# Splitting float64 weights: the sign carried by a parametric ReLU and a bound on GpSimd, instead of a pass on VectorE

## Chip, core and metric

The kernel runs on one core of a Trainium2 chip. The metric is the device time of one execution in microseconds (us); smaller is better.

## What is computed

A scan over chunks of 32 steps (4 batches, 8 heads, 768 steps, head dimension 32, state 16), and behind it two feed-forward layers on 3072 tokens, 256 to 2048 to 256:

```python
y   = scan(x, a, B, C)                      # per head: CB * decay on the chunk, state between chunks
x   = y.transpose(0, 2, 1, 3).reshape(3072, 256)
h   = x @ w_in;  g = np.maximum(0.01 * h, h);  x = g @ w_out
h   = np.maximum(x @ w2_in, 0.0);              out = h * h @ w2_out
```

The four weight matrices arrive as float64, 512 Ki numbers each. The kernel reads them as 64-bit words and makes two float32 parts of each number itself, a high part that TensorE takes as it is and a low part that is the rest.

## The kernel before

**Scan.** The work is cut into 12 pieces of 256 steps. `scan_piece` computes one: scaled fp16 parts of its inputs on ScalarE and VectorE, block-diagonal copies (`diag`), products on TensorE (lines 340, 341, 365 to 367, 385, 386), running products on VectorE (lines 188, 194, 212). Its last two steps give the tokens of the feed-forward layers: `yh` on ScalarE (line 389) and then `yl` on VectorE (line 390), the instruction that the first matmuls of a block wait for.

**Feed-forward.** The tokens stand in 8 blocks of one or two pieces, and `ORDER` lists the 16 phases (layer and block: first layer of block 0, of 1, of 2, second layer of block 0, and so on). In each phase `Phase.hmm` multiplies with two or one 128-column parts of the first matrix (lines 417 to 419), `act` applies the nonlinearity on ScalarE (lines 427, 428 or 430, 432) and VectorE (line 431, and `gl` in line 433), and `omm` multiplies with the second matrix, one to three rounds later (lines 445, 446, 450).

**Weights.** The four matrices are split into 8 chunks each, 32 in all; a chunk is 128 partitions x 512 numbers. `w_step` moves four chunks on by one stage each:

- `load_w` (line 120): a DMA from SP's queue into a buffer `wst` of 64-bit words.
- `split_w`: two ScalarE instructions in place. Line 129 multiplies the upper word, read as float32, by 2 to the -112, which rebases the exponent; line 132 turns the lower word into the last bits of the fraction.
- `split_w1`: two VectorE instructions in place. Line 140 shifts the scaled upper word left by 3 and puts it over the lower word; line 141 puts the sign bit of the upper word over that, since the shift has pushed it out.
- `split_w2`: the high part on ScalarE (line 152), the low part on VectorE (line 153).

```python
nc.scalar.activation(w1.bitcast(F32), w1.bitcast(F32), AF.Copy, scale=2.0**-112)                       # 129
nc.vector.scalar_tensor_tensor(w0, w1, 3, w0, ALU.logical_shift_left, ALU.bitwise_or)                  # 140
nc.vector.scalar_tensor_tensor(w0, w1, -(1 << 31), w0, ALU.bitwise_and, ALU.bitwise_or)                # 141
```

Eight `w_step`s are written ahead of the first block; the rest is spread over the phases. In which order the instructions stand on each engine is decided at build time by a scheduler with a cost table of its own; each engine then runs its list in order, and waits by semaphores. GpSimd only sets up constants at the start (lines 68 to 88).

Of the kernel before, what the change touches and what calls it, by code (L numbers as in the profile page):

```python
# [8 lines left out]
F32 = mybir.dt.float32  # L9
F32R = mybir.dt.float32r  # L10
F16 = mybir.dt.float16
I32 = mybir.dt.int32
I64 = mybir.dt.int64
U32 = mybir.dt.uint32
AF = mybir.ActivationFunctionType
ALU = mybir.AluOpType
# [28 lines left out]
def ssd_moe_kernel(ctx: ExitStack, tc: tile.TileContext, in1, in2, w1i, w1o, w2i, w2o, out):  # L45
# [6 lines left out]
    nc = tc.nc  # L52
# [18 lines left out]
    nc.scalar.activation(lr, ones, AF.Lrelu)  # L71
    delta = cp.tile([P, U, T], F16, name="delta")


    xbh = cp.tile([P, U, 4, T], F16, name="xbh")
    xbl = cp.tile([P, U, 4, T], F16, name="xbl")
    kbd = cp.tile([P, U, 4, T], F16, name="kbd")
    sbd = cp.tile([P, U, 4, T], F16, name="sbd")
    d1e = cp.tile([P, U, T], F32, name="d1e")
# [30 lines left out]
    def load_w():  # L110
        nm, c = wq.pop(0)
        if nm == "2o" and c >= 5:
            st = yp.tile([P, 2, 256], I64, tag="y2", name="wst")
        else:
            st = wp.tile([P, 2, 256], I64, tag="w", name="wst")
        if nm[1] == "i":
            sl = (slice(None), slice(None), slice(c * 256, c * 256 + 256))
        else:
            sl = (slice(None), slice(2 * c, 2 * c + 2), slice(None))
        nc.sync.dma_start(st, w_dram[nm][sl])  # L120
        w_loaded.append((nm, c, sl, st))

    def split_w():
        nm, c, sl, st = w_loaded.pop(0)
        v = st.bitcast(I32).rearrange("p k (f two) -> p k f two", two=2)
        w0, w1 = v[:, :, :, 0], v[:, :, :, 1]


        nc.scalar.activation(w1.bitcast(F32), w1.bitcast(F32), AF.Copy, scale=2.0**-112)


        nc.scalar.activation(
            w0, w0.bitcast(U32), AF.Copy, scale=2.0**-29 * (1 - 2.0**-14), bias=7.5 * 2.0**-14 - 0.5
        )
        w_half.append((nm, c, sl, w0, w1))

    def split_w1():

        nm, c, sl, w0, w1 = w_half.pop(0)
        nc.vector.scalar_tensor_tensor(w0, w1, 3, w0, ALU.logical_shift_left, ALU.bitwise_or)  # L140
        nc.vector.scalar_tensor_tensor(w0, w1, -(1 << 31), w0, ALU.bitwise_and, ALU.bitwise_or)  # L141
        w_full.append((nm, c, sl, w0.bitcast(F32)))

    def split_w2():
# [10 lines left out]
    def w_step():  # L155
        if w_full:
            split_w2()
        if w_half:
            split_w1()
        if w_loaded:  # L160
            split_w()
        if wq:
            load_w()
# [61 lines left out]
    def piece_scales(p, tiles):  # L225
# [16 lines left out]
        iss = sm.tile([P, 1], F32, tag="iss", name="iss", bufs=3)  # L242
        nc.vector.tensor_single_scalar(er.bitcast(I32), rb.bitcast(I32), MASK, ALU.bitwise_and)
        nc.vector.tensor_scalar(ss.bitcast(I32), er.bitcast(I32), -1.0, 268.0 * E23, ALU.mult, ALU.add)
        nc.vector.tensor_scalar(iss.bitcast(I32), er.bitcast(I32), -14.0 * E23, None, ALU.add)
        kk = sm.tile([P, 1], F32, tag="kk", name="kk")
# [30 lines left out]
    def powers(mx):  # L277
# [14 lines left out]
        nc.vector.tensor_scalar(eb, Sf[:, P : P + 3], 2.0**-50, None, ALU.max)  # L292
        nc.vector.tensor_single_scalar(eb.bitcast(I32), eb.bitcast(I32), MASK, ALU.bitwise_and)
        nc.vector.tensor_scalar(sc.bitcast(I32), eb.bitcast(I32), -1.0, 267.0 * E23, ALU.mult, ALU.add)
        nc.vector.tensor_scalar(isc.bitcast(I32), eb.bitcast(I32), -13.0 * E23, None, ALU.add)
# [4 lines left out]
    def scan_piece(p, tiles, get_y):  # L300
# [12 lines left out]

        him = sp.tile([P, U, T], F16, tag="f0", name="him")
        ch = sp.tile([P, U, T], F16, tag="f2", name="ch")
# [174 lines left out]
    for _ in range(W_AHEAD):  # L490
        load_w()
# [120 lines left out]
```

## Time and profile before

| what | value |
|---|---|
| median of 3 runs | 652.51 us (652.01 to 653.04) |
| profiled execution, first to last instruction (span) | 647.8 us |
| median less that span | 4.7 us |
| busy in the span: TensorE (PE), VectorE (DVE) | 592.5 us, 420.4 us |
| busy in the span: ScalarE (ACT), GpSimd (POOL) | 356.9 us, 5.1 us |
| mean granted clock of TensorE | 0.989 |

The profile gives one execution, and of its time the span alone. Times in it count from the span's start. SP only issues DMAs. A busy TensorE is one with a matmul in flight; the start-to-start distance of its matmuls says at which of its two clock levels it works.

### The profile page before, as it was taken

What the parts mean: (1) busy time and instruction counts of PE and PEld (TensorE: products, weight loads), DVE (VectorE), ACT (ScalarE), POOL (GpSimd) and SP (SyncE); (2) the same over time, 40 slices, a digit from 0 to 9 for tenths busy, and PEclk for the clock granted to TensorE, in tenths of its full rate; (3) what the DMA queues carried; (4) which work ended last, traced back from release to release, by engine and by line L of the source; (5) the groups of instructions that cost most, each with busy time, mean ns of one, the idle gap of its engine ahead of it and who ended that gap; (6) DMA issues with size and microseconds to landing.
All of it is one profiled execution on the core that took longest, in us unless ns stands there. A gap on an engine that the chain in (4) does not pass through costs nothing.

```text
span 647.8 us, 11305 instructions
## 1 busy us (share of the span) xinstructions
PE 592.5 (91%) x4440; PEld 514.8 (79%) x4440; DVE 420.4 (65%) x726; ACT 356.9 (55%) x630; POOL 5.1 (1%) x14
## 2 busy tenths in 40 slices
PE   0278695999999999999999999999999999999997
PEld 0177595999999988899987888888888888788885
DVE  7989999898768854576554586563565322554553
ACT  5999776665555545545535555455544433544442
POOL 3000000000000000000000000000000000000000
PEclk9999898899999999999999999999999999999999
DMA  9775765423635422202212212212000000000000
GB/s 323 240 242 136 238 138 150 127 61 65 172 33 149 76 73 24 50 34 42 50 50 25 50 33 25 50 66 25 8 1 10 33 0 1 0 1 2 32 2 32
DMA packets 111397, 46.48 MB, mean 72 GB/s; under 512 B 94320, under 2 KB 101104, under 8 KB 111344
## 3 DMA queue, kind: packets, MB, share of 16 engines
q1 hardware_dynamic: 111344, 45.76, 27.2%
q8 instruction: 35, 0.57, 0.4%
q14 instruction: 18, 0.15, 0.1%
HBM read 36.83 MB, written 3.15 MB: 62 GB/s over the span
## 4 chain that ended last, share of the span: by engine, by line
PE 72%; DVE 16%; ACT 4%; DMA 4%; issue 3%; SPq 0%; DVEq 0%; ACTq 0%
PE o L445 12%; PE hp L417 12%; PE hp L419 12%; PE hp L418 11%; PE o L446 11%; PE o L450 11%; DMA all<-in 3%; DVE gl L433 2%; DVE wst L140 2%; DVE wst L141 2%; DVE t L431 1%; DVE mx L266 1%; DVE e L194 1%; DVE lt L188 1%; DVE wl1i L153 1%
## 5 line engine op out<-in xcount | busy, mean ns | idle before, releaser
L433 DVE TENSOR_TENSOR gl<-t,gh 128x512 fp32r<-128x512 f32 x192 | 132.0, 688 | 130.1 <-ACT t L428 80.4
L427 ACT ACTIVATE gh<-hp 128x512 fp32r<-128x512 f32 x96 | 57.2, 596 | 95.4 <-PE o L446 77.8
L432 ACT CAST gh<-t 128x512 fp32r<-128x512 f32 x96 | 59.6, 621 | 74.8 <-DVE t L431 64.5
L417 PE MATMUL hp<-yl,wh1i 128*128 128x256 f32 (+1 forms) x256 | 89.4, 349 | 9.5 <-DVE yl L390 9.5
L431 DVE TENSOR_TENSOR t<-t 128x512 f32<-128x512 f32 x96 | 66.1, 688 | 44.5 <-ACT t L430 44.4
L418 PE MATMUL hp<-yh,wh1i 128*128 128x256 f32 (+1 forms) x256 | 88.8, 347 | 0.0
L419 PE MATMUL hp<-yh,wl1i 128*128 128x256 f32 (+1 forms) x256 | 88.8, 347 | 0.0
L430 ACT ACTIVATE t<-hp 128x512 f32<-128x512 f32 x96 | 57.3, 597 | 57.2 <-PE hp L419 54.6
L445 PE MATMUL o<-gh,wl1o 128*128 128x256 f32 (+1 forms) x256 | 84.8, 347 | 3.6 <-DVE wl1o L153 3.4
L417 PE MATMUL hp<-yl,wh2i 128*128 128x256 f32 (+1 forms) x256 | 86.8, 339 | 0.0
L419 PE MATMUL hp<-yh,wl2i 128*128 128x256 f32 (+1 forms) x256 | 86.5, 338 | 0.0
L418 PE MATMUL hp<-yh,wh2i 128*128 128x256 f32 (+1 forms) x256 | 86.2, 337 | 0.0
L445 PE MATMUL o<-gh,w2o 128*128 128x256 f32 (+1 forms) x256 | 83.6, 343 | 2.1 <-DVE yl L459 1.9
L446 PE MATMUL o<-gh,wh1o 128*128 128x256 f32 (+1 forms) x256 | 82.8, 339 | 0.0
L446 PE MATMUL o<-gh,w2o 128*128 128x256 f32 (+1 forms) x256 | 81.7, 336 | 0.0
L417 PEld LDWEIGHTS hp<-yl,wh1i 128*128 128x128 f32 x256 | 50.7, 198 | 15.1 <-issue 5.8
L450 PE MATMUL o<-gl,wh1o 128*128 128x256 f32 (+1 forms) x256 | 61.1, 339 | 0.6 <-DVE gl L433 0.6
L450 PE MATMUL o<-gl,w2o 128*128 128x256 f32 (+1 forms) x256 | 60.8, 337 | 0.0
L445 PEld LDWEIGHTS o<-gh,wl1o 128*128 128x128 f32 x256 | 48.2, 188 | 12.0 <-DVE wl1o L153 5.8
L428 ACT ACTIVATE t<-hp 128x512 f32<-128x512 f32 x96 | 56.9, 593 | 0.0
L419 PEld LDWEIGHTS hp<-yh,wl1i 128*128 128x128 f32 x256 | 50.6, 198 | 5.9 <-issue 0.2
L418 PEld LDWEIGHTS hp<-yh,wh1i 128*128 128x128 f32 x256 | 50.8, 198 | 5.4
(124 smaller groups left out, 982.1 us busy)
## 6 DMA issues: line engine op xcount, KB each, us to landing
in<-in SPq DMA_DIRECT2D x12, 640.0 KB, 4.5
in<-in SPq DMA_DIRECT2D x12, 512.0 KB, 3.3
all<-in SPq DMA_DIRECT2D x15, 384.0 KB, 3.7
wst<-w1i SPq DMA_DIRECT2D x8, 512.0 KB, 9.2
wst<-w1o SPq DMA_DIRECT2D x8, 512.0 KB, 4.6
wst<-w2o SPq DMA_DIRECT2D x8, 512.0 KB, 5.7
wst<-w2i SPq DMA_DIRECT2D x8, 512.0 KB, 5.0
out_t<-ob SPq DMA_DIRECT2D x8, 256.0 KB, 2.2
```

The costliest lines, as they stand in the source:

```text
L417: nc.tensor.matmul(hp, wh, self.xl[:, :, k], start=(k == 0), stop=False)
L418: nc.tensor.matmul(hp, wh, self.xh[:, :, k], start=False, stop=False)
L419: nc.tensor.matmul(hp, wl, self.xh[:, :, k], start=False, stop=(k == KI - 1))
L427: nc.scalar.activation(gh, hp, AF.Lrelu)
L428: nc.scalar.activation(t, hp, AF.Lrelu)
L430: nc.scalar.activation(t, hp, AF.Relu)
L431: nc.vector.tensor_tensor(t, t, t, ALU.mult)
L432: nc.scalar.copy(gh, t)
L433: nc.vector.tensor_tensor(gl, t, gh.bitcast(F32), ALU.subtract)
L445: nc.tensor.matmul(self.o[d], wl, gh, start=(m == 0), stop=False)
L446: nc.tensor.matmul(self.o[d], wh, gh, start=False, stop=False)
L450: nc.tensor.matmul(self.o[d], wh, gl, start=False, stop=(m == KO - 1))
```

## The change

The sign pass (line 141) is removed. To let the sign through the shift, line 129's Copy becomes a Prelu: a positive upper word is scaled by 2 to the -112 as before, a negative one by -(2 to the -80), so that it comes out positive with an exponent larger by 32, a bit that the left shift by 3 brings to the sign's place. So that tiny negative numbers don't fall out of that range, an instruction on GpSimd, issued behind the load of each chunk, bounds the upper 16 bits of every upper word from below, as a signed 16-bit number, in place.

```diff
+I16 = mybir.dt.int16
@@ load_w
         nc.sync.dma_start(st, w_dram[nm][sl])
+
+
+        top = st.bitcast(I16).rearrange("p k (f four) -> p k f four", four=4)[:, :, :, 3]
+        nc.gpsimd.tensor_single_scalar(top, top, (113 << 7) - (1 << 15), ALU.max)
         w_loaded.append((nm, c, sl, st))
@@ split_w
-        nc.scalar.activation(w1.bitcast(F32), w1.bitcast(F32), AF.Copy, scale=2.0**-112)
+        nc.scalar.activation(w1.bitcast(F32), w1.bitcast(F32), AF.Prelu, scale=2.0**-112, alpha=-(2.0**32))
@@ split_w1
         nc.vector.scalar_tensor_tensor(w0, w1, 3, w0, ALU.logical_shift_left, ALU.bitwise_or)
-        nc.vector.scalar_tensor_tensor(w0, w1, -(1 << 31), w0, ALU.bitwise_and, ALU.bitwise_or)
         w_full.append((nm, c, sl, w0.bitcast(F32)))
```

The scheduler makes another order of it. In the order of the change the lines of the program stand 1 further up to line 120 and 4 further from line 124 to 141, and again 4 behind that (the new instruction is line 125, the Prelu line 134, the other ScalarE step line 137, the shift line 145, the parts lines 156 and 157).

VectorE at the head, from the reduction that makes `pm` on. Before:

```order
L84 TENSOR_REDUCE pm<-ident 128x1
L140 SCALAR_TENSOR_TENSOR wst<-wst 128x512
L282 TENSOR_REDUCE m_134<-S 3x1
L141 SCALAR_TENSOR_TENSOR wst<-wst 128x512
L284 TENSOR_SCALAR dg<-ident,m_134 3x3
L140 SCALAR_TENSOR_TENSOR wst<-wst 128x512
L292 TENSOR_SCALAR eb<-S 128x3
L153 TENSOR_TENSOR wl1i<-wst,wh1i 128x2x256
```

And in the change:

```order
L85 TENSOR_REDUCE pm<-ident 128x1
L286 TENSOR_REDUCE m_138<-S 3x1
L288 TENSOR_SCALAR dg<-ident,m_138 3x3
L296 TENSOR_SCALAR eb<-S 128x3
L297 TENSOR_SCALAR eb<-eb 128x3
L298 TENSOR_SCALAR sc<-eb 128x3
```

The steps of the scan's scales (`m`, `dg`, `eb`, `sc`) now follow each other; the first shift of a weight chunk stands 26 rows behind `pm`.

ScalarE at the head, with what each instruction waits for, from the copy of `dec` on. Before:

```order
L195 COPY dec<-e_181 128x32x8 [waits DVE_49]
L129 ACTIVATE wst<-wst 128x512 [waits DMAHW2_49]
L132 ACTIVATE wst<-wst 128x512
L129 ACTIVATE wst<-wst 128x512 [waits DMAHW3_49]
...
L152 ACTIVATE wh1i<-wst 128x2x256 [waits DVE_49]
...
L317 ACTIVATE ch<-in_116,sc 128x512 [waits DMAHW0_49,DVE_49]
```

And in the change:

```order
L199 COPY dec<-e_185 128x32x8 [waits DVE_49]
L137 ACTIVATE wst<-wst 128x512 [waits DMAHW2_49]
L137 ACTIVATE wst<-wst 128x512 [waits DMAHW3_49]
L321 ACTIVATE ch<-in_116,sc 128x512 [waits DMAHW0_49,DVE_49]
...
L362 ACTIVATE qh<-e_185,sc 128x512
L134 ACTIVATE wst<-wst 128x512 [waits Pool_49]
L356 CAST mkh<-in_117 128x768 [waits DVE_49]
```

The scan's first inputs (`ch`) are made after two weight instructions instead of eight, and the first Prelu, which waits for GpSimd, comes only behind `qh`.

GpSimd, whose list ended with `dec` before, has 32 more rows in the change, one for each chunk, in the order of the loads. The first of them:

```order
L89 MEMSET dec 128x32 [waits Pool_49]
L125 TENSOR_SCALAR wst<-wst 128x512 [waits DMAHW2_49]
L125 TENSOR_SCALAR wst<-wst 128x512 [waits DMAHW3_49]
L125 TENSOR_SCALAR wst<-wst 128x512 [waits DMAHW4_49]
L125 TENSOR_SCALAR wst<-wst 128x512 [waits DMAHW5_49]
```

Each waits for the DMA of its chunk.

## Rows read from the trace of the kernel before

**Rows 1.** The page's first part: busy us, share of the span, instructions.
```profile
PE 592.5 (91%) x4440; PEld 514.8 (79%) x4440; DVE 420.4 (65%) x726; ACT 356.9 (55%) x630; POOL 5.1 (1%) x14
```

**Rows 2.** Busy us by stretch (from:to), with instructions, granted clock, DMA.
```profile
core 0: us, PE busy (x) PEld busy (x) DVE busy (x) ACT busy (x) POOL busy (x), PEclk, DMA share, GB/s
...
8.00:37.00 29.00, 5.21 (x115) 4.76 (x116) 27.59 (x62) 27.90 (x48) 0.00 (x0) 1.00 0.83 291
37.00:48.00 11.00, 10.76 (x75) 10.18 (x75) 9.45 (x23) 9.69 (x19) 0.00 (x0) 1.00 0.64 215
48.00:72.00 24.00, 18.73 (x203) 17.09 (x201) 23.96 (x48) 21.93 (x41) 0.00 (x0) 1.00 0.59 155
72.00:90.00 18.00, 15.11 (x162) 14.49 (x161) 17.04 (x41) 14.42 (x28) 0.00 (x0) 0.91 0.71 198
90.00:122.00 32.00, 23.47 (x237) 22.56 (x236) 29.57 (x59) 20.35 (x38) 0.00 (x0) 0.84 0.57 146
122.00:150.00 28.00, 26.70 (x286) 26.36 (x285) 27.79 (x47) 19.26 (x36) 0.00 (x0) 1.00 0.28 74
150.00:300.00 150.00, 148.19 (x1395) 137.26 (x1394) 102.71 (x170) 78.86 (x142) 0.00 (x0) 1.00 0.32 73
```

**Rows 3.** TensorE's waits over the span: us in total, times, longest us.
```profile
PE hp L417 <- DVE yl L390: 9.5, 3, 5.7
...
PE o L445 <- DVE wl1o L153: 3.4, 3, 1.5
```

**Rows 4.** TensorE in order of time: start us, us, instruction [idle before].
```profile
36.64 0.58 PE L417 MATMUL hp<-yl,wh1i 128*128 128x256 f32 x1 [2.22 <-DVE yl L390]
...
40.42 0.28 PE L417 MATMUL hp<-yl,wh1i 128*128 128x256 f32 x1
40.54 0.28 PE L418 MATMUL hp<-yh,wh1i 128*128 128x256 f32 x1
...
114.29 0.55 PE L417 MATMUL hp<-yl,wh1i 128*128 128x256 f32 x1 [5.72 <-DVE yl L390]
114.64 0.42 PE L418 MATMUL hp<-yh,wh1i 128*128 128x256 f32 x1
...
118.27 0.41 PE L417 MATMUL hp<-yl,wh1i 128*128 128x256 f32 x1
```

**Rows 5.** Groups by line: count | busy us, mean ns | idle before us.
```profile
L427 ACT ACTIVATE gh<-hp 128x512 fp32r<-128x512 f32 x96 | 57.2, 596 | 95.4 <-PE o L446 77.8 <-PE hp L419 17.4
...
L132 ACT ACTIVATE wst<-wst 128x512 int32<-128x512 uint32 x32 | 21.8, 680 | 0.0
L129 ACT ACTIVATE wst<-wst 128x512 f32<-128x512 f32 x32 | 21.7, 678 | 0.2
L141 DVE SCALAR_TENSOR_TENSOR wst<-wst 128x512 int32<-128x512 int32 x32 | 21.7, 680 | 0.0
```

**Rows 6.** VectorE in order of time, at 20 us.
```profile
20.80 0.69 DVE L141 SCALAR_TENSOR_TENSOR wst<-wst 128x512 int32<-128x512 int32 x1
21.40 0.74 DVE L350 SCALAR_TENSOR_TENSOR in<-S,kk,lt 128x512 f32<-128x512 f32 x1
```

**Rows 7.** GpSimd in order of time, and ScalarE's table load from its own list.
```profile
1.14 0.29 POOL masks.py:199 TENSOR_SCALAR_AFFINE_SELECT ident<-ident 128x128 f32<-128x128 f32 x1
1.38 0.95 POOL L83 MEMSET kbd<- 128x1024 f32 x1
...
3.17 2.55 POOL L87 CAST delta<-ident 32x512 f16<-32x512 f32 x4
...
0.73 1.28 ACT L71 ACT_TABLE_LOAD   x1 [0.73 <-PEq L602]
```

**Rows 8.** VectorE's scale reductions of the first two pieces, in order of time.
```profile
4.85 1.61 DVE L229 TENSOR_REDUCE mx<-in 128x1 f32<-128x256 f32 x3 [1.24 <-DMA in<-in]
...
39.80 0.42 DVE L229 TENSOR_REDUCE mx<-in 128x1 f32<-128x256 f32 x1
...
41.33 1.27 DVE L229 TENSOR_REDUCE mx<-in 128x1 f32<-128x512 f32 x2
```

## Prediction

> **What bounds the kernel now.** I read four views in this order: busy time by engine, busy time by stretch, TensorE's waits, and the rows of single engines where those waits end. Over the whole span TensorE leads: 592.5 of 647.8 us, against 420.4 on VectorE, 356.9 on ScalarE and 5.1 on GpSimd [rows 1]. That average hides two regimes [rows 2]. From 150 us on TensorE is full (148.2 of 150), so nothing done there to the other engines can show. Before that it is not: between 8 and 37 us it has almost nothing to do, and from 37 to 150 us it is busy 94.8 of 113 us. In all of 8 to 150 us VectorE is nearly full (27.6 of 29, 9.5 of 11, 24.0 of 24, 17.0 of 18, 29.6 of 32, 27.8 of 28), and ScalarE is nearly full only up to 72 us (27.9 of 29, 9.7 of 11, 21.9 of 24). All 32 weight chunks are split in this part, so the change lies wholly where VectorE is the bound, and whatever TensorE gains there stays gained, since it is the bound afterwards.
>
> TensorE's waits say where the gain can come in [rows 3]. The largest are for `yl`, VectorE's last step of a scan piece, 9.5 us in 3 waits: 2.2 us ahead of the first block at 36.64 us, 5.7 us ahead of the block at 114.29 us, the rest between. For the low part of `w1o` it waits 3.4 us. A wait costs twice: of the 18 matmuls from 114.64 to 118.27 us, right behind the longest one, one starts every 0.21 us, elsewhere every 0.12 us [rows 4], which goes with the two clock levels, 1.2 and 2.4 GHz (the granted clock of 72 to 90 and 90 to 122 us is 0.91 and 0.84, of most other stretches 1.00).
>
> **What goes.** 32 sign passes on VectorE, 680 ns each [rows 5]. Such operations start every 0.60 us when they follow each other (20.80, then 21.40 us [rows 6]), so each frees 0.60 us: 32 x 0.60 = 19.2 us, all of it between 8 and 150 us. No wait cost is saved with them: VectorE was not idle ahead of line 141 [rows 5].
>
> **What is changed in place.** The Copy of line 129 becomes a Prelu with a constant slope: 32 x 678 ns before [rows 5]. Nothing shows a Prelu here; the nearest rows are the Lrelu of line 427 at 596 ns, which reads PSUM, and the plain Copy of line 132 at 680 ns, within 90 ns of each other [rows 5]. I take no change; 32 x 0.09 = 3 us of ScalarE time would be the end on the bad side, half of it in the stretch where ScalarE is full. The order of the change still has a single table load, so none of 1.28 us [rows 7] is added.
>
> **What is added.** 32 operations on GpSimd, 128x512 of 16 bits, one in and one out of SBUF. GpSimd has nothing to do behind 8 us [rows 2]. No row shows this operation. Nearest is the CAST of line 87, 512 elements per partition, four in 2.55 us, 0.64 us each. Ends from other rows: a MEMSET of 1024 elements in 0.95 us gives 0.48 us for 512; an AFFINE_SELECT of 128 elements in 0.29 us gives 1.17 us for 512 [rows 7]. I take 0.64 us. The queue is then filled 32 x 0.64 = 20.5 us of 140 (at 1.17 us 37 us), so GpSimd is no bound by itself.
>
> Each adds a wait: line 134's Prelu on ScalarE comes behind it, and the shift on VectorE behind that. A chunk is ready up to 0.64 us later than its landing allows. The queue of ScalarE would stand still then, with scan work behind the Prelu. But the built order puts 3 weight Copies and the whole first scan batch ahead of the first Prelu, and chunks land well ahead of use, so I cost this at nothing; without that cover it is 0.64 us for the 9 chunks of the head, 6 us at the worst.
>
> **What moves.** Counting the built order ahead of the first `yl`: before, 24 weight operations on VectorE (9 first shifts, 8 sign passes, 7 low parts); now 12 (7 and 5), and three scale reductions of the next piece (1.7 us, [rows 8]) have come ahead of it. That is 12 x 0.60 - 1.7 = 5.5 us less on VectorE; on ScalarE 28 weight operations become 19, 9 x 0.68 = 6 us less at the most [rows 5]. Ahead of the `yl` of the third piece (113.4 us) VectorE had 67 weight operations and has 51: 16 x 0.60 = 9.6 us less. These are the two places where TensorE starts a block late.
>
> **What GpSimd takes back.** This is the unknown that decides. In the only stretch of the trace where GpSimd works, VectorE runs reductions with one input: three take 1.61 us beside the CAST, and 0.42 + 1.27 = 1.69 us later with GpSimd idle [rows 8], so nothing is lost there. But almost all of VectorE's work from 8 to 150 us has two tensor inputs (lines 140, 153, 433 and the scans), and no row shows such an operation beside a busy GpSimd. Bounds: 0, from that row; and the whole of each GpSimd operation, 0.64 us, if one engine stands while the other reads. I take the middle, 0.32 us, since neither row excludes either end: 32 x 0.32 = 10.2 us given back of 19.2.
>
> **The sum.** At the head some 9 GpSimd operations fall ahead of the first `yl`: 5.5 - 9 x 0.32 = 2.6 us earlier. Ahead of the third `yl` some 27: 9.6 - 8.6 = 1.0 us net, so this place keeps the head's gain no more than partly; at the end of the weight work 19.2 - 10.2 = 9.0 us less has been done on VectorE, which stage 122 to 150 us can hardly use, TensorE being busy 26.7 of 28 there. Between, the three waits for `w1o` (3.4 us) have two operations before them instead of three. I put the result between 1.0 and 9.0 us, at 5 us: the span 647.8 becomes 642.8, and with the 4.7 us that lie between this profiled span and the median of the runs, 652.5 becomes **647.5 us**.
>
> **Rivals.**
> *GpSimd takes nothing back.* For it: the reductions beside the CAST [rows 8]. Against it: they have one input. Then VectorE gains 5.5 us at the head and 9.6 us up to the third piece; the 5.7 us wait shrinks away and with it the 18 matmuls at the low clock behind it (18 x 0.09 = 1.6 us, [rows 4]). 9.6 + 1.6 = 11.2 us, ScalarE at 59.5 of 64 us up to 72 us allows hardly more: **641 us**. If the head's gain adds fully, 638.
>
> *Slower: the two engines shut each other out.* VectorE's two-input operations follow each other without a gap; if a GpSimd operation holds what they need for its whole length, each of the 32 costs VectorE that length, and GpSimd and behind it ScalarE's Prelu wait for a gap in turn. The point from which it decides is 0.60 us per operation: at 0.64 us it is 20.5 against 19.2, a loss of 1.3 us, at 0.9 us (midway between 0.64 and 1.17) 28.8 against 19.2, a loss of 9.6 us. Up to the third `yl` the balance is worse, 27 x 0.64 - 9.6 = 7.7 us at the short length. With TensorE's own idle time partly absorbing it: +2 to +10, **657 us**. At 1.17 us it is 37.4 - 19.2 = 18 us, 671. For it: of the three lengths worked out above, two are over the break-even; against it: nothing in the trace shows it.
> The Trainium skill, page "SBUF — State Buffer", section "Who interferes with whom", speaks for this rival: a VectorE instruction with two SBUF inputs and a GpSimd instruction that reads SBUF exclude each other for a whole instruction, whichever comes second standing still. No row here shows it; by it alone the sum would be this rival's.
>
> *No change.* The freed time falls where ScalarE is full (8 to 72 us) and TensorE is full (from 122 us): 652.5.
>
> *The change does not do what it says:* Prelu brings table loads, 64 x 1.28 = 82 us. The built order has none; 0.01.
>
> **How the numbers follow.** Forecast, 644 to 651: 0.35. Nothing taken back, 637 to 644: 0.27. Slower, 654 to 671: 0.29. No change: 0.08. Faster by over 0.2% (1.3 us, about what the measurement can tell) takes the first two less a little: 0.61; within 0.2%: 0.10; slower: 0.29. The range reaches down over nearly all of the second case and up over the slower one without the long GpSimd operation: 638 to 661 us. The likeliest case's own range is 644 to 651.
>
> **What would show it.** Line 141 gone, VectorE's busy time down by 32 x 0.68 = 22 us if nothing is taken back; if it falls by less, or the mean of its other two-input operations rises, that is what GpSimd takes. The GpSimd rows' spacing tells their length. The first matmul of `Phase.hmm` should start near 34 us; at 31 us the first rival holds, at 37 or later the second. The wait of 5.7 us for `yl` should be shorter and the granted clock of 90 to 122 us above 0.84. I am wrong at the root if the first `yl` comes later although 12 weight operations fewer stand ahead of it, or if ScalarE's waits for GpSimd add up to more than a few us.

## The result and the profile after

The change takes 657.94 us (median of 4 runs, 657.25 to 658.89); the kernel before, run beside it, 652.47 us (4 runs). The ratio of after to before is 1.0094 with a 95% interval of 1.0078 to 1.0109: slower by 0.8 to 1.1%, some 5.5 to 6 us. The forecast was 647.5 us; the time lies in the range of 638 to 661, on the other side of no change.

Busy time by engine of the kernel after the change answers to [rows 1]:

```profile
PE 595.0 (91%) x4440; PEld 516.9 (79%) x4440; DVE 417.9 (64%) x694; ACT 357.5 (55%) x630; POOL 86.7 (13%) x46
```

VectorE (DVE) has 32 instructions fewer, 694 for 726, and yet its busy time fell by only 2.5 us, from 420.4. GpSimd (POOL) rose from 5.1 to 86.7 us. The span is 655.5 us, 7.7 more than before; TensorE is busy 2.5 us longer and stands idle for the other 5.2.

The same stretches as in [rows 2], in the same columns, after the change:

```profile
8.00:37.00 29.00, 4.77 (x114) 4.48 (x114) 27.25 (x48) 20.97 (x35) 24.16 (x10) 1.00 0.66 224
37.00:48.00 11.00, 8.64 (x57) 7.74 (x54) 11.00 (x22) 10.16 (x18) 11.00 (x5) 1.00 0.89 294
48.00:72.00 24.00, 20.10 (x210) 18.27 (x210) 23.47 (x44) 21.34 (x40) 17.26 (x8) 1.00 0.60 170
72.00:90.00 18.00, 10.59 (x92) 9.86 (x93) 16.52 (x40) 16.12 (x32) 11.48 (x5) 0.72 0.57 150
90.00:122.00 32.00, 25.29 (x281) 24.34 (x280) 29.30 (x55) 20.86 (x37) 7.98 (x3) 0.88 0.55 134
122.00:150.00 28.00, 28.00 (x289) 27.91 (x289) 23.43 (x35) 21.31 (x39) 9.66 (x4) 0.96 0.51 163
150.00:300.00 150.00, 145.95 (x1368) 135.47 (x1367) 99.58 (x166) 77.74 (x139) 0.00 (x0) 0.99 0.31 69
```

In the first row, from 8 to 37 us, VectorE is as full as before (27.25 us for 27.59) and gets through 48 instructions instead of 62. ScalarE, full before (27.9), is now busy 21.0 us: in this stretch it waits for VectorE, 3.2 us once for `in` and 2.7 us once for the scales `sc`. Matmuls done by 300 us, added up over these rows and the one up to 8 us, are 2413 where they were 2475: 62 fewer, at 0.11 us each (150 us by 1395, [rows 2]) about 7 us, nearly the whole 7.7 us of the span. Of the 62, 35 are missing by 150 us and the other 27 behind it, where TensorE waits 3.3 us once for line 463, the low part of what the first layer hands to the second (named `yl` too). So the loss is made in the weight phase and just behind it, and carried to the end. The granted clock shares in it: from 72 to 90 us, around the longest wait for the scan's `yl` (5.3 us, below), it is 0.72 where it was 0.91.

Groups by line, which answer to [rows 5] (the columns are the same):

```profile
L125 POOL TENSOR_SCALAR wst<-wst 128x512 int16<-128x512 int16 x32 | 81.5, 2667 | 57.9 <-DVE d1s L208 16.9 <-DVE gl L437 16.5 <-DMA wst<-w2o 9.1
L145 DVE SCALAR_TENSOR_TENSOR wst<-wst 128x512 int32<-128x512 int32 x32 | 22.8, 719 | 1.7 <-ACT wst L134 1.4 <-issue 0.3
L137 ACT ACTIVATE wst<-wst 128x512 int32<-128x512 uint32 x32 | 22.4, 706 | 1.1 <-DMA wst<-w1i 0.5 <-DMA wst<-w2o 0.5
L134 ACT ACTIVATE wst<-wst 128x512 f32<-128x512 f32 x32 | 21.6, 681 | 1.9 <-POOL wst L125 1.9
```

The Prelu of line 134 takes 681 ns, as the Copy it replaces (678). The new bound of line 125 takes 2667 ns on average, where the prediction had 640. Two rows of GpSimd in order of time:

```profile
8.49 15.37 POOL L125 TENSOR_SCALAR wst<-wst 128x512 int16<-128x512 int16 x7 [2.60 <-DMA wst<-w1i]
28.21 4.43 POOL L125 TENSOR_SCALAR wst<-wst 128x512 int16<-128x512 int16 x1 [4.35 <-DMA wst<-w1i]
```

Seven bounds in 15.37 us, 2.2 us each, and a single one that took 4.43 us while VectorE worked beside it. VectorE in the same stretch, in order of time:

```profile
16.50 0.72 DVE L327 SCALAR_TENSOR_TENSOR kmx<-in,sc,him 128x512 f16<-128x512 f32 x1
17.15 1.11 DVE L337 SCALAR_TENSOR_TENSOR xl<-in,sc,xh 128x512 f16<-128x512 f32 x1
18.18 1.89 DVE L316 COPY kbd<-kmx 32x512 f16<-32x512 f16 x2
20.10 1.62 DVE L316 COPY xbh<-xh 32x512 f16<-32x512 f16 x2
...
34.16 1.75 DVE L316 COPY sbd<-t 32x512 f16<-32x512 f16 x2
...
38.94 0.74 DVE L394 SCALAR_TENSOR_TENSOR yl<-Y,fac,yh 128x512 fp32r<-128x512 f32 x1
```

The same two steps in the kernel before, a pair of copies and the first `yl`:

```profile
18.58 0.57 DVE L312 COPY xbh<-xh 32x512 f16<-32x512 f16 x2
...
35.84 0.75 DVE L390 SCALAR_TENSOR_TENSOR yl<-Y,fac,yh 128x512 fp32r<-128x512 f32 x1
```

Two block-diagonal copies (line 316) take 1.6 to 1.9 us, for 0.57. Of the two-input products just ahead of them, line 327 takes 0.72 us and line 337 takes 1.11. The first `yl` starts at 38.94 us, 3.1 us later than before, though VectorE has 12 weight operations fewer ahead of it. TensorE's waits for `yl` and for line 463, and ScalarE's for GpSimd, from the waits over the span:

```profile
PE hp L421 <- DVE yl L394: 10.7, 3, 5.3
...
PE o L449 <- DVE yl L463: 3.3, 1, 3.3
...
ACT wst L134 <- POOL wst L125: 1.9, 1, 1.9
```

The wait for `yl` grew from 9.5 to 10.7 us [rows 3]. Its sum is no measure of the loss: in a run below that is faster than the kernel before it is 10.3 us.

### The profile page after: what moved, and what is told of

It reads as the page before. It is cut to its first block, busy times and chain, and to the rows that moved or that the text cites. A ratio compares the mean times of both kernels' runs of the same rounds, so it can differ in the third digit from the quotient of the medians.

```text
span 655.5 us, 11371 instructions
## 1 busy us (share of the span) xinstructions
PE 595.0 (91%) x4440; PEld 516.9 (79%) x4440; DVE 417.9 (64%) x694; ACT 357.5 (55%) x630; POOL 86.7 (13%) x46
## 4 chain that ended last, share of the span: by engine, by line
PE 75%; DVE 12%; ACT 5%; DMA 4%; issue 2%; SPq 0%; POOLq 0%; DVEq 0%; ACTq 0%
PE o L449 12%; PE hp L421 12%; PE hp L423 12%; PE hp L422 12%; PE o L454 12%; PE o L450 12%; DMA wst<-w2o 2%; DVE gl L437 1%; DMA all<-in 1%; ACT wst L134 1%; DVE wst L145 1%; DVE e L198 1%; ACT wst L137 1%; DVE lt L192 1%; PE Y L389 1%
## 5 line engine op out<-in xcount | busy, mean ns | idle before, releaser
L421 PE MATMUL hp<-yl,wh1i 128*128 128x256 f32 (+1 forms) x256 | 89.7, 350 | 10.7 <-DVE yl L394 10.7
L125 POOL TENSOR_SCALAR wst<-wst 128x512 int16<-128x512 int16 x32 | 81.5, 2667 | 57.9 <-DVE d1s L208 16.9
L421 PEld LDWEIGHTS hp<-yl,wh1i 128*128 128x128 f32 x256 | 51.0, 199 | 16.6 <-issue 10.2
L449 PEld LDWEIGHTS o<-gh,w2o 128*128 128x128 f32 x256 | 48.2, 189 | 10.2 <-DVE yl L463 3.9
```

Of the source, the lines that this page charges most:

```text
L125: nc.gpsimd.tensor_single_scalar(top, top, (113 << 7) - (1 << 15), ALU.max)
L421: nc.tensor.matmul(hp, wh, self.xl[:, :, k], start=(k == 0), stop=False)
L449: nc.tensor.matmul(self.o[d], wl, gh, start=(m == 0), stop=False)
```

## The experiments

In these, the time is told as the ratio to the kernel before on the same chip, and a difference between two kernels as the difference of their ratios times 652.5 us; with intervals of 0.15 to 0.3% to either side of each, such a difference is good to about 2 us.

**Leave the bound out.** The change without GpSimd's instruction:

```diff
-        top = st.bitcast(I16).rearrange("p k (f four) -> p k f four", four=4)[:, :, :, 3]
-        nc.gpsimd.tensor_single_scalar(top, top, (113 << 7) - (1 << 15), ALU.max)
```

> The change without the 32 GpSimd instructions (so negative weights below about 2^-119 in magnitude would lose their sign; the rest is computed as in the change). Theory A, GpSimd's instructions hold up VectorE: without them VectorE's busy time falls by the 21.7 us of the sign passes to about 399 us, no one-input VectorE instruction is longer than before, and the time falls below the kernel before, to 638 to 646 us. Theory B, the removal of the sign pass is worth little because ScalarE and the scan chain hold the first 72 us: 650 to 653 us. Theory C, the Prelu itself or the order of the scan steps makes the loss: still above 655 us.

Measured: 643.04 us, ratio 0.9883 (0.9860 to 0.9906), 7.6 us faster than before and 13.8 us faster than the change. The engines' busy time in this kernel:

```profile
PE 593.7 (93%) x4440; PEld 516.8 (81%) x4440; DVE 402.6 (63%) x694; ACT 355.7 (55%) x630; POOL 5.1 (1%) x14
```

VectorE is at 402.6 us, 17.8 below before: this is what the sign passes were worth to it, 0.56 us each. (The 399 us expected had put each at its own length, 0.68 us.) The 15.3 us up to the 417.9 of the change come and go with the GpSimd instruction.

**Add the bound alone.** The kernel before, with only the two lines above added:

> The kernel before with the 32 GpSimd instructions added and nothing else changed (Copy and sign pass stay). Theory A: the whole price of GpSimd without the gain, VectorE's busy time 435 to 442 us, the time 660 to 672 us, that is above the change. Theory B: the price is small, 652 to 656 us. Theory C (Prelu or its place): 652 us.

Measured: 668.68 us, ratio 1.0274 (1.0245 to 1.0304), 17.9 us slower than before. Its busy time:

```profile
PE 600.9 (90%) x4440; PEld 522.3 (78%) x4440; DVE 437.7 (66%) x726; ACT 359.1 (54%) x630; POOL 82.2 (12%) x46
```

The same 726 instructions on VectorE are 17.3 us longer. So the bounds take about as much from VectorE with the sign passes as without (15.3 us); in time they cost 17.9 us here and 13.8 in the change.

**Price each pairing.** A kernel that does nothing but this: on idle engines first GpSimd's bound, the same on 16-bit and on 32-bit numbers without a step, then VectorE's operations alone, and then each of them beside four bounds, with a barrier between the stages. It leaves out the computation; the outputs are zeros. Shortened, without the barriers:

```python
bound(4); flat16(4); flat32(4)                          # GpSimd alone, 512 elements per partition
shift(12); subtract(12); copy16(16); clip(12); tiny(16); reduce(8)      # VectorE alone
for op, n in ((shift, 16), (subtract, 16), (copy16, 16), (clip, 16), (tiny, 16), (reduce, 12)):
    bound(4); op(n)                                     # side by side
```

> Prices by themselves; none of the reference is computed, zeros are written. GpSimd's bound alone: theory A about 2.06 us from start to start, the shortest distance in the change; if its length came from waiting for VectorE it would be 0.6 to 0.7 us alone. The same 16-bit maximum on contiguous words and a float32 maximum show whether the stride or the 16-bit type makes the length. Beside GpSimd: if only one-input instructions with both operands in SBUF are held up, the copies, clips and tiny instructions of VectorE get longer by up to 2 us each, and shift, subtract (two inputs) and reductions keep 0.60 us; if two-input instructions exclude GpSimd, shift and subtract get longer too or GpSimd's own distance grows above 2.6 us.

GpSimd in order of time: the bound, the two without a step, and the four beside the shifts and beside the copies.

```profile
23.83 8.33 POOL L54 TENSOR_SCALAR g<-g 128x512 int16<-128x512 int16 x4 [23.40 <-SPq L95]
32.35 5.84 POOL L59 TENSOR_SCALAR q<-q 128x512 int16<-128x512 int16 x4 [0.20 <-SPq L97]
38.39 5.84 POOL L63 TENSOR_SCALAR q<-q 128x512 f32<-128x512 f32 x4 [0.20 <-SPq L99]
72.89 9.46 POOL L54 TENSOR_SCALAR g<-g 128x512 int16<-128x512 int16 x4 [28.67 <-SPq L113]
...
96.02 9.41 POOL L54 TENSOR_SCALAR g<-g 128x512 int16<-128x512 int16 x4 [2.15 <-SPq L117]
```

Alone, a bound takes 8.33 / 4 = 2.08 us; 512 elements that lie side by side take 1.46 us, with 16 bits as with 32. VectorE in order of time, alone (44 to 73 us) and beside the bounds:

```profile
44.30 7.31 DVE L68 SCALAR_TENSOR_TENSOR w<-w 128x512 int32<-128x512 int32 x12 [32.00 <-SPq L101]
...
59.09 3.31 DVE L76 COPY k<-h 32x512 f16<-32x512 f16 x16
62.48 4.01 DVE L80 TENSOR_SCALAR c<-a 128x496 f32<-128x496 f32 x12
...
67.93 4.83 DVE L88 TENSOR_REDUCE f<-a 128x1 f32<-128x512 f32 x8
72.84 11.47 DVE L68 SCALAR_TENSOR_TENSOR w<-w 128x512 int32<-128x512 int32 x16
...
95.89 8.36 DVE L76 COPY k<-h 32x512 f16<-32x512 f16 x16
105.51 11.48 DVE L80 TENSOR_SCALAR c<-a 128x496 f32<-128x496 f32 x16 [1.25 <-SPq L117]
...
125.69 7.21 DVE L88 TENSOR_REDUCE f<-a 128x1 f32<-128x512 f32 x12 [5.64 <-SPq L117]
```

Sixteen shifts, the two-input operation of the weight path, would take 16 / 12 x 7.31 = 9.75 us alone and take 11.47 beside four bounds: 0.43 us lost per bound. The fp16 copies lose (8.36 - 3.31) / 4 = 1.26 us per bound at the least, since they end at 104.25 us and the fourth bound at 105.43; the one-input clip loses (11.48 - 16 / 12 x 4.01) / 4 = 1.53 us, the reductions nothing (12 / 8 x 4.83 = 7.25). Neither reading put ahead of the run holds alone: one-input and two-input operations both get longer, and GpSimd's bound grows to 9.46 / 4 = 2.37 us beside the shifts. The prediction looked for the danger in the two-input operations; copies and clips pay three times as much per bound.

The Trainium skill, page "SBUF — State Buffer", section "Who interferes with whom", says that a VectorE instruction in a two-port mode (copies and tensor_scalar can be), or one with two SBUF inputs, and a GpSimd instruction that reads SBUF block each other for a whole instruction, and that reductions do not. For reductions the run agrees (7.21 us, 7.25 alone). For the two-input shift it does not: 0.43 us are lost of 2.08, and shifts and bounds together took 11.5 us, where one after the other they would take 9.75 + 8.33 = 18.1. For copies and clips 1.26 and 1.53 us are lost, not the whole either.

**The bound on VectorE.** The change with the same instruction issued on VectorE:

```diff
-        nc.gpsimd.tensor_single_scalar(top, top, (113 << 7) - (1 << 15), ALU.max)
+        nc.vector.tensor_single_scalar(top, top, (113 << 7) - (1 << 15), ALU.max)
```

> The change with the bound issued on VectorE instead of GpSimd, everything else the same. A 512-element one-input instruction there costs between 0.33 us (clip of 496 float32 in 0.41 us is the nearest row, 0.34 us from start to start) and 0.60 us (the sign pass that it replaces). Theory A: no GpSimd, so no instruction of VectorE gets longer, and the time is that of the kernel before less 0 to 9 us of VectorE's work, 645 to 652 us. Theory C: above 655 us again.

Measured: 653.65 us, ratio 1.0038 (1.0023 to 1.0054), slower than both the kernel before and the 645 to 652 us expected. Its group:

```profile
L125 DVE TENSOR_SCALAR wst<-wst 128x512 int16<-128x512 int16 x32 | 23.5, 740 | 1.4 <-DMA wst<-w1i 1.0 <-DMA wst<-w1o 0.4
```

VectorE's busy time is 419.0 us, 16.4 above the run without a bound, 0.51 us for each. That is about what a sign pass costs (17.8 / 32 = 0.56), so nearly nothing is left to gain. The time is even 2.5 us worse than before, with VectorE 1.4 us less busy; why is not shown (this kernel has an order of its own, and the bound still stands between a chunk's load and its Prelu). Against the run without a bound the bounds cost 10.1 us here. It is 3.7 us better than with the bound on GpSimd, which keeps VectorE about as busy (417.9).

**Order or bound.** Each of these kernels gets its own order from the scheduler, so the runs so far mix two things. In the next five, the order of every instruction on TensorE, VectorE, ScalarE and SP is fixed by edges that cost no semaphore, to a listed one:

```python
for a, b in zip(places, places[1:]):
    tc.add_manual_dep(
        mine[b],
        mine[a].name,
        mybir.DependencyInfo(mybir.DependencyClass.NoSync, mybir.DependencyReason.DATA),
        reason="as listed",
    )
```

First the order of the change, with the bound cut to 8 of each 512 words, so that every wait stays and the work goes:

```diff
+        top = top[:, 0:1, 0:8]
         nc.gpsimd.tensor_single_scalar(top, top, (113 << 7) - (1 << 15), ALU.max)
```

> The change with every engine's order kept as the change has it, but each GpSimd bound cut to 8 of its 512 words per partition (so most tiny negative weights are not bounded). Theory A, GpSimd's instructions hold up VectorE: most of the loss goes, 642 to 648 us, and no one-input VectorE instruction is longer than before. Theory O, the order that the scheduler built around a slow GpSimd (scan steps first, the eighth load of w1i and those of w1o late) makes the loss: 654 us or more, as the change itself.

Measured: 642.82 us, ratio 0.9868 (0.9845 to 0.9891): 8.6 us faster than before, 14.7 us faster than the change. Its busy time, VectorE at the head, and TensorE's wait for `yl`:

```profile
PE 594.4 (93%) x4440; PEld 517.0 (81%) x4440; DVE 402.8 (63%) x694; ACT 356.1 (56%) x630; POOL 19.7 (3%) x46
```

```profile
27.98 0.57 DVE L342 COPY sbd<-t 32x512 f16<-32x512 f16 x2
31.58 0.74 DVE L420 SCALAR_TENSOR_TENSOR yl<-Y,fac,yh 128x512 fp32r<-128x512 f32 x1
```

```profile
PE hp L447 <- DVE yl L420: 10.3, 3, 4.9
```

The same instructions in the same order: the copies are back at 0.57 us for two, the first `yl` stands at 31.58 us instead of 38.94. With the order equal, the groups of VectorE can be subtracted, the change less this kernel. The single durations grow by 16.8 us in all (15.1 in busy time, since neighbours overlap a little): two-input operations carry 6.4, tensor_scalar operations 5.5, the copies 4.6, the scans 0.4, the reductions 0.0. By share of their own time the copies grow by two thirds, the tensor_scalar operations by two fifths, the two-input operations, most of which run behind the last bound, by 2%. The copies and one-input operations suffer most, as in the pairing run.

Then the opposite, the full bound in the order of the run that has none:

> The change in full, GpSimd's bounds included, with the order of all other engines that the scheduler built for the run without bounds. Theory A: the bounds bring back what they took, 655 to 661 us, about as the change. Theory O: the better order keeps most of that run's gain, 643 to 649 us.

Measured: 656.14 us, ratio 1.0077 (1.0050 to 1.0105). The bound costs 12.7 us in this order and 14.7 in its own: the two differ by 2 us, about what such a difference is good to, so the scheduler's new order is not to blame. Here VectorE loses less (412.3 us, 9.7 above the run without), and ScalarE waits more:

```profile
ACT wst L159 <- POOL wst L150: 11.9, 9, 3.4
```

That row is the second part of the price, late chunks. In its own order the change hides it (1.9 us): the Prelus were put later, not sooner.

**Which bounds cost.** The order of the change, with the small bound for the 8 chunks of the first matrix and the full one for the other 24:

> The change with its order kept, the bound full for 24 chunks and cut to 8 of 512 words for the 8 chunks of w1i, those split before the first block. If the loss is made where the scan of the first piece stands alone on the way to the first matmul, the time falls by at least a third of what the run with all bounds cut gains; if each bound costs the same wherever it stands, by a quarter of it.

Measured: 652.39 us, ratio 1.0018 (1.0002 to 1.0034). The 8 bounds of the head cost 5.0 us (1.0094 less 1.0018), the other 24 cost 9.8: 0.6 and 0.4 us for each. The 5.0 us are 34% of 14.7, and at 2 us to either side they do not decide between the third and the quarter of the expectation. Its busy time says more:

```profile
PE 595.8 (92%) x4440; PEld 518.1 (80%) x4440; DVE 410.1 (63%) x694; ACT 356.5 (55%) x630; POOL 70.9 (11%) x46
```

VectorE is 7.8 us below the change, so the 8 bounds of the head take about 1 us each from it, and the other 24, with the remaining 7.3 us, 0.3 each. Those 24 cost more time (9.8 us) than they take from VectorE, which its slowing alone does not explain.

**Slowing or lateness.** Two runs in the order of the change take the two parts by themselves. In the first GpSimd works as long, on a spare tile, and nobody waits for it:

```diff
-        top = st.bitcast(I16).rearrange("p k (f four) -> p k f four", four=4)[:, :, :, 3]
-        nc.gpsimd.tensor_single_scalar(top, top, (113 << 7) - (1 << 15), ALU.max)
+        for half in range(2):
+            idle = spare.bitcast(I16).rearrange("p (f four) -> p f four", four=4)[:, :, 3]
+            nc.gpsimd.tensor_single_scalar(idle, idle, (113 << 7) - (1 << 15), ALU.max)
```

> The order of the change on TensorE, VectorE, ScalarE and SP, but no bound on the weights (negative weights other than zero below about 2 to the -119 in size would come out wrong). In its place GpSimd works 64 times on 224 words of a spare tile, with the same 8-byte step, behind each other from about 6 us on and with nobody waiting for them; if two of them take what one bound did (2.06 us), they end near 72 us. Theory one, that what the bounds cost is the slowing of VectorE's instructions beside them: VectorE's busy time rises by 12 to 20 us over the 402.8 of the run with the small bound, and the time is 654 to 661 us. Theory two, that the cost is that chunks become ready later and ScalarE and VectorE stand behind them: 642 to 646 us. Between 647 and 653 both have a part.

Measured: 649.33 us, ratio 0.9963 (0.9948 to 0.9977): 6.2 us slower than with the small bound, in the stretch where both theories were to have a part. Its busy time, GpSimd's pieces, and the first `yl`:

```profile
PE 593.9 (92%) x4440; PEld 516.3 (80%) x4440; DVE 411.3 (63%) x694; ACT 356.7 (55%) x630; POOL 90.9 (14%) x79
```

```profile
6.35 90.64 POOL L153 TENSOR_SCALAR spare<-spare 128x224 int16<-128x224 int16 x64
```

```profile
31.30 1.17 DVE L344 COPY sbd<-t 32x512 f16<-32x512 f16 x2
35.67 0.73 DVE L422 SCALAR_TENSOR_TENSOR yl<-Y,fac,yh 128x512 fp32r<-128x512 f32 x1
```

VectorE is 8.5 us longer, the first `yl` 4.1 us later. No instruction of another engine waits for GpSimd's new work here, so slowing alone costs time. The pieces take longer than expected, 1.42 us each, and end at 97 us instead of 72. It is weaker than in the change (8.5 us for 15.1): the short pieces on the spare tile double the copies, where the bounds triple them.

In the second the chunks come late, and GpSimd spends the time between landing and ready mostly in writing a spare tile, without reading:

```diff
-        nc.gpsimd.tensor_single_scalar(top, top, (113 << 7) - (1 << 15), ALU.max)
+        rest = (top[:, 0:1, 8:16], top[:, 0:1, 16:24], top[:, 0:1, 24:32]) if (nm, c) == ("2o", 5) else (None, None, None)
+        for some in (top[:, 0:1, 0:8], *rest, top[:, 1:2, 0:8]):
+            if some is None:
+                nc.gpsimd.memset(spare, 0.0)
+            else:
+                nc.gpsimd.tensor_single_scalar(some, some, (113 << 7) - (1 << 15), ALU.max)
```

(One chunk, whose load comes out of turn, has three small bounds in place of the fills.)

> The order of the change on TensorE, VectorE, ScalarE and SP. In each chunk GpSimd bounds 8 of the 512 words, then fills a spare tile three times (0.47 us each), then bounds 8 words more, and the Prelu waits for the last of the five: some 2.1 to 2.3 us from landing to ready, as with the full bound, but with an instruction that only writes in most of it (the other words are not bounded; negative weights other than zero below about 2 to the -119 in size would come out wrong there). VectorE's busy time tells whether the fills slow it: if it stays near 402.8, the time is the price of the later chunks alone. Theory one, the cost is the slowing of VectorE's instructions: 642 to 645 us. Theory two, the cost is the later chunks: 650 to 658 us. The run with bounds that nobody waits for gave 649.3, so a third reading is that the two add up: then about 648 to 652 here. If VectorE's busy time rises by more than 5 us, the run tells nothing.

Measured: 648.65 us, ratio 0.9973 (0.9956 to 0.9990): 6.9 us slower than with the small bound, where the third reading was put. Its busy time, then GpSimd's first chunk, the first `yl` on VectorE, and ScalarE's wait for GpSimd:

```profile
PE 593.6 (92%) x4440; PEld 516.3 (80%) x4440; DVE 405.2 (63%) x694; ACT 357.0 (55%) x630; POOL 83.4 (13%) x174
```

```profile
8.11 0.24 POOL L172 TENSOR_SCALAR wst<-wst 128x8 int16<-128x8 int16 x1 [2.21 <-DMA wst<-w1i]
8.28 1.53 POOL L170 MEMSET spare<- 128x448 f32 x3
```

```profile
33.11 0.74 DVE L441 SCALAR_TENSOR_TENSOR yl<-Y,fac,yh 128x512 fp32r<-128x512 f32 x1
```

```profile
ACT wst L181 <- POOL wst L172: 3.1, 4, 1.5
```

VectorE is 2.4 us longer. At the rate of the run before (6.2 us of time for 8.5 of VectorE's) that would be 1.8 us, an estimate; the other 5 us are put down to lateness: a chunk is handed on at least 1.9 us after the one before it (8.11 us and 8.28 + 1.53, with a small bound behind), whatever has landed. As waits of ScalarE for GpSimd only 3.1 us of it can be seen. The two parts, 6.2 and 6.9 us, add up to 13.1 of the 14.7 us. How the change divides its own 14.7 between them is not settled: its bounds slow VectorE more than the first of the two runs does (15.1 us for 8.5), and 2.4 us of slowing are in the second.

## Why the prediction was wrong

**What bounds the kernel: right in the main.** From 8 to 122 us VectorE is as full in the change (107.5 of 114 us), and what is lost there is not won back: TensorE is 62 matmuls behind at 300 us. From 122 to 150 us it is TensorE that is full in the change (28.0 of 28).

**What goes: right.** 19.2 us were put down for the sign passes; VectorE's busy time fell by 17.8 and 17.6 us in the two runs where nothing or next to nothing takes their place. The 22 us that the prediction named as a sign (32 x 0.68) were never to come by its own 0.60 us. In time these runs gain 7.6 and 8.6 us, where the first rival had 11.2 us (641 us); its other end, 638, is not what it is said to be made of, since 11.2 and 5.5 us off 652.5 are 636.

**What is changed in place: right.** 681 ns for 678.

**What is added: the step that failed first.** The bound was put at 0.64 us, from the CAST of line 87 [rows 7], and at most at 1.17. It takes 2.08 us alone and 2.67 beside VectorE. The row was the nearest in size and not in kind: its output lies side by side on 32 partitions, while the bound steps 8 bytes on 128. The step explains 2.08 against 1.46 us; what sets 1.46 against 0.64 for the CAST no run tells.

**The added wait: it failed as well.** "I cost this at nothing; without that cover it is 0.64 us for the 9 chunks of the head, 6 us at the worst." The cover was the built order, which puts other work ahead of the first Prelu. It does cover ScalarE's queue (1.9 us of waits after the change). It does not cover the pace: the chunks go one by one through an engine that needs 2.2 us and more for each, and the run that has lateness nearly alone is 6.9 us slower, some 5 us of it by the estimate above.

**What GpSimd takes back: mis-sized.** 0.32 us per bound were taken, between 0 and 0.64. The two kernels with the same order give (417.9 - 402.8) / 32 = 0.47 us. So GpSimd takes back 15.1 us, not 10.2, of the 17.6 that the sign passes left. That reductions lose nothing was read rightly, from a thin row: they run from 4.85 to 6.46 us, and the CAST beside them ends at 3.17 + 2.55 = 5.72 [rows 7, rows 8]; the pairing run shows it for whole bounds. Taking only the two-input operations for the ones at risk was half right: a bound costs them 0.43 us, and in the kernel they lose 6.4 of the 16.8 us, but it costs the copies and clips 1.26 to 1.53, and these and the other tensor_scalar operations lose 10.1.

**What moves: right without GpSimd.** 5.5 us less work ahead of the first `yl` was counted; with the small bound it starts at 31.58 us, 4.3 us earlier than before (35.84). "I am wrong at the root if the first `yl` comes later although 12 weight operations fewer stand ahead of it" was the test, and it is what the change showed. Two other signs did not tell the cases apart: as for a faster kernel, the longest wait for `yl` shrank (5.3 us for 5.7) and the granted clock from 90 to 122 us rose (0.88 for 0.84).

**The sum with the measured terms.** In VectorE's busy time, 17.6 us off and 15.1 back leave 2.5 us. In the kernel's time, the run with the small bound is 8.6 us faster, and the two runs that take the parts by themselves give back 6.2 and 6.9 us: 4.5 us slower, against 5.5 to 6 measured. Each of these two runs is still faster than before (ratios 0.9963 and 0.9973), so as strong as they have it neither part turns the sign alone. Whether the change's own slowing would is not shown: 15.1 us at the rate of 6.2 for 8.5 are 11 us, an estimate, which is more than 8.6.

**The rivals.** "Slower: the two engines shut each other out" named the time, 657 us, for a mechanism that is half of it. Its break-even, 0.60 us per operation, was not reached on VectorE (0.47, with 0.55 freed by each pass); the rest is put down to the wait, which it mentions in passing. The rule of the Trainium skill, page "SBUF — State Buffer", section "Who interferes with whom", with VectorE standing for the whole of each bound at the length measured alone, would have given back 32 x 2.08 = 67 us, an estimate, where 15.1 were. *GpSimd takes nothing back* is the case of the runs with no bound or a small one. TensorE's wait for `w1o` nearly went, as the forecast had it:

```profile
L449 PE MATMUL o<-gh,wl1o 128*128 128x256 f32 x128 | 32.8, 289 | 2.0 <-ACT gh L431 1.7 <-DVE wl1o L157 0.3
```

This is the group of the first `o` products after the change: 0.3 us behind `wl1o`, where it was 3.4 us [rows 3].

## What to carry to other kernels

Work moved to an idle engine has two prices beside its own length: what it takes from the engine beside it, by the kind of operation that runs there (here, GpSimd beside VectorE, 0 for reductions, 0.4 us for two-input operations, 1.3 to 1.5 us for fp16 copies and fp32 clips, per bound of 2.08 us), and the pace at which it hands things on to a stage that is the bound. Before taking a duration from a row, look whether the row has the same step; if none has, let the range reach as far as a slower form would cost. Here the version to keep drops the bound altogether (643 us, 1.2% faster than before). By its arithmetic it gives the same result as long as no weight is a negative number closer to zero than about 2 to the -119 and yet not zero; no run tried such weights.

## What was not expected of the hardware

- Line 125's bound of 512 16-bit numbers at an 8-byte step takes 2.08 us with the other engines idle, 1.46 without the step, and the same 1.46 us for 512 numbers of 32 bits: the width does not count, the step does.
- On VectorE the same instruction takes 0.51 us of the engine's time: a quarter.
- The slowing goes both ways. The bound rose from 2.08 to 2.37 us beside the shifts and to a mean of 2.67 in the kernel, where one took 4.43 us.
- A GpSimd instruction that only writes still slows the copies: in the run with fills, two `kbd` copies took 1.15 us, nearly all of it beside three fills, against 0.57 for two with the small bound:

```profile
15.26 1.55 POOL L170 MEMSET spare<- 128x448 f32 x3
```

```profile
15.81 1.15 DVE L363 COPY kbd<-kmx 32x512 f16<-32x512 f16 x2
```
